# Three of a block's sums of silu(h) on GpSimd, early, in a convolution + silu MLP kernel

## The chip, the cores and the metric

One NeuronCore of a Trainium2 chip. The metric is device time in microseconds of one execution of the whole program; the number to compare is the median of the runs. PE is TensorE, DVE VectorE, ACT ScalarE, POOL GpSimd, SP SyncE (here it only issues DMAs).

## What is computed

The reference, cut to what matters (fp32 throughout):

```python
# x: (8, 4096, 192); weight: (8 heads, 7 taps)
w = softmax(weight, axis=-1)
x_pad = concat([zeros(B, 6, D), x], axis=1)
conv[b, s, h, g] = sum_k w[h, k] * x_pad[b, s + k, h, g]      # causal, 7 taps
x = conv.reshape(32768, 192)
h = x @ w_in                                                  # 192 -> 2048
g = h * (1.0 / (1.0 + np.exp(-h)))                            # silu
out = g @ w_out                                               # 2048 -> 192
```

## The kernel before, in words

**Blocks.** The 32768 tokens are worked on in 32 blocks of 1024 (two halves n of 512). A block goes through: load (`ld`, DMA), transposing into channels by tokens (`i`, DVE), the left edge (`ha`), the convolution (`v`), spreading of its result to other partitions (`sp`, DMA), differences of the spread tiles (`w`, DVE), the products with w_in (`P`, `L`, PE), sums that turn products into h (`u`, `X`, `a`, `b`), silu (`S`, `SL`, ACT), sums of silu(h) (`t`), the products with w_out (`D`, PE), sums of those (`M`, `z`, `y`, `x`), transposing back (`o`) and storing (`st`).

**Products.** Both matrix products use a scheme with fewer multiplications, in which inputs are first added or subtracted and the products are added afterwards. For w_in there are five groups g of 15 products each; P5.2 is product 5 of group 2. A product uses 64 of the 128 rows, so two run at once. Each group has three PSUM banks in which products are added one after another (chains, `CHAINS` in line 618: the first is 5, 2, 6, 1, 0, 14) and two more banks (x banks). Between two products of the first chain ACT copies the bank's present value into an SBUF tile (u5.2 is the copy behind P5.2, in line 698), and the next product of the chain is then added to the same bank, so it waits until the copy has read it. DVE adds such a copy to the second chain's bank: into an x bank (`X`), or into h (`a`), and subtracts the third (`b`), all in line 692. X2.2 is followed by P13.2, which adds to that x bank. `S` applies silu (line 710): S0, S1 and S5 work in place on h in SBUF, S2, S3 and S4 read PSUM. All these run in the first half of a block's time; the w_out products (`D`, line 765, 48 of them) fill the other half.

**The sums of silu(h).** For each quarter j of the 2048 features there are four (lines 718 to 733), 16 in a block, each of 128 x 1024 elements in fp32, both inputs and the output in SBUF. With g(a, n) the silu values of chunk a and half n: t.j0 = g(0,1) - g(0,0); t.j1 = g(1,1) - t.j0; t.j2 = g(1,1) - g(0,1); t.j3 = g(1,0) - t.j1. For j = 0, t.00 reads the results of S0.0, S4.0, S1.0 and S5.0; t.01 and t.02 read those of S3.0 and S1.4 as well. D1 and D0 need no sum; D2.00 is the first that reads t.01, D4.01 and D5.00 read t.00, D3.00 reads t.02. The results go into tiles of the pool `t`, which has three buffers of 128 x 2048.

**The convolution of a later block** runs between all this. For each of three channel groups k and seven taps, `v.k0` is a scaled copy on ACT into the tile nat; `v.k1` to `v.k6` (lines 509 to 513) are a scaled copy on ACT into one of ten tiles u, then a DMA, issued from POOL's queue, that adds that tile to nat. The ten tiles are handed out in the order in which they came back (list `free`): `v` takes one and puts it back at once, `u` takes one and `X` or `a` puts it back. Whoever writes a tile next waits for its last reader, for instance that DMA.

**Order.** Each engine executes in program order. That order is written out by hand in the string `PLAN`, one token after the other for one block, gone through once for each iteration; `-`, `=` and `+` before a token mean one block earlier, two earlier, one later. So in iteration b, `+v.21` is tap 1 of group 2 of the convolution whose result is needed two blocks later, `-t.00` is a sum of the block before. `START` is the same for the first planned blocks (iteration 2), whose w_out products of block 0 run in another form. `finish` (line 937) ends the last block. A k-th instruction of an engine in the trace can thus be matched with a token.

Around the change, PLAN reads (token, engine): S4.4, S0.0 (ACT), +v.21 (ACT, then a DMA from POOL), P5.2 (PE), u5.2 (ACT), P14.4, S3.4, P1.1, u0.1, P13.1, S2.1, P8.4, a0.4 (DVE), P5.3, u5.3, sp.1 (DMA from SP), P2.2 and so on. SP issues, in the same stretch, one of the four DMAs of `sp.1`, three of `-st.1` (stores) and four of `-ld.1` (loads).

```python
    def used(*key):                                   # line 682
        free.append(us.pop(key))
...
            z = free.pop(0)                           # line 510, conv, taps 1 to 6
            pin(nc.scalar.activation(z, src, AF.Copy, scale=tap))
            pin(nc.gpsimd.dma_start(out=dst, in_=z, accum_op=ALU.add))
            free.append(z)
```

Of the kernel before, what the change touches and what calls it, by code (L numbers as in the profile page):

```python
# [12 lines left out]
ALU = mybir.AluOpType  # L13
# [4 lines left out]
def kernel(  # L18
# [24 lines left out]
    nc = tc.nc  # L43
# [36 lines left out]

    PLAN = (
# [21 lines left out]
    )  # L103
    START = (
# [39 lines left out]
    )  # L144
    QUEUE = (0, 4, 1, 2, 3)
    CHAIN_BANKS = (
# [20 lines left out]
    def pin(ins):  # L167
        return tc.keep_in_program_order(ins)
# [37 lines left out]
    x0 = x.flatten_outer_dims()[TB - pad : TB, :].rearrange("t (k c) -> c k t", k=NK)  # L206
# [511 lines left out]
    def sum_g(b, j, i):  # L718

        t = sums.setdefault((b, j), {})  # L720
        if i // 2 not in t:
            t[i // 2] = tpool.tile([P, 2, 2 * TB], F32, tag="t", name="t")

        def of(a, n):
            return gs[b, j, a][:, n, :, :].rearrange("p e t -> p (e t)")

        u, v = (
            (lambda: (of(0, 1), of(0, 0))),
            (lambda: (of(1, 1), t[0][:, 0, :])),
            (lambda: (of(1, 1), of(0, 1))),  # L730
            (lambda: (of(1, 0), t[0][:, 1, :])),
        )[i]()
        pin(nc.vector.tensor_tensor(t[i // 2][:, i % 2, :], u, v, op=ALU.subtract))  # L733

    def out_slot(b, j, i, e, half=None):

# [145 lines left out]
    def step(b, token):  # L882
# [19 lines left out]
        elif name[0] in "uXabS":  # L902
            sums_h(b, name, *digits)
        elif name == "t":
            sum_g(b, *digits)
        elif name[0] == "D":
            i, (j, e) = int(name[1]), digits
            for half in range(2) if i == 3 and b == NB - 1 else (None,):
                out_slot(b, j, i, e, half)
        elif name[0] in "Mzyx":  # L910
            merge(b, name, *digits)
        elif name == "o":
            turn_out(b, *digits)
        elif name == "st":
            store_out(b, *digits)
        elif name == "dp":
            next(downs)
        elif name == "cp":
            copy_plain(b, *digits)
        elif name == "go":  # L920
            pool.tensor_copy(warm, nats[1][:, digits[0], 0, 0:1])
            for g in (2, 3):
                for e in range(2):
                    combine(g, e)
        elif name == "ld":
            if b + 1 < NB:
                load(b + 1, digits)
        elif b + 1 < NB:
            {"i": turn_in, "ha": halo_in, "v": conv, "sp": spread, "w": win}[name](
                b + 1, *digits[: 1 + (name == "v")]  # L930
            )
# [204 lines left out]
```

## Time and profile before

| what | value |
|---|---|
| median of 2 runs | 2319.99 us (2319.82 to 2320.15) |
| the profiled execution's span | 2317.9 us, 2.1 us under that median |
| PE, DVE, ACT, POOL busy | 2310.2, 1797.9, 1496.0, 534.9 us |
| a steady block (P5.1 to the next block's P5.1) | 71.19 us |
| granted TensorE clock, mean | 1.000 |
| sums of silu(h) on DVE, `t<-g`, x248 | mean 1216 ns |
| sums of silu(h) on DVE, `t<-g,t`, x248 | mean 1223 ns |
| silu in place, `g<-g` on ACT, x465 | mean 629 ns |
| convolution DMAs from POOL, `nat<-u`, x504 | mean 947 ns on POOL, landing after 4.5 us (median) |

How to read it: a line of a timeline gives the start in us, the length in us, the engine, the line of the kernel, the operation, output<-input by the program's names, partitions x elements, how many instructions were merged, and in brackets how long the engine had sat idle ahead of it and what ended that. A line of the list of groups gives busy us, mean ns of one, and idle us before them. A matmul's start is the start of its stream; its end is modelled. "Landing" is the time from a DMA's start on its queue to the last of its semaphore updates. An fp32 matmul shows as two instructions. All times in us are counted from the start of the span; most are from the block with u5.2 at 1260.64.

### The profile page before, as it was taken

What the parts mean: (1) busy time and instruction counts of PE and PEld (TensorE: products, weight loads), DVE (VectorE), ACT (ScalarE), POOL (GpSimd) and SP (SyncE); (2) the same over time, 40 slices, a digit from 0 to 9 for tenths busy, and PEclk for the clock granted to TensorE, in tenths of its full rate; (3) what the DMA queues carried; (4) which work ended last, traced back from release to release, by engine and by line L of the source; (5) the groups of instructions that cost most, each with busy time, mean ns of one, the idle gap of its engine ahead of it and who ended that gap; (6) DMA issues with size and microseconds to landing.
All of it is one profiled execution on the core that took longest, in us unless ns stands there. A gap on an engine that the chain in (4) does not pass through costs nothing.

```text
span 2317.9 us, 45421 instructions
## 1 busy us (share of the span) xinstructions
PE 2310.2 (100%) x17630; PEld 949.6 (41%) x17630; DVE 1797.9 (78%) x2373; ACT 1496.0 (65%) x2779; POOL 534.9 (23%) x675
## 2 busy tenths in 40 slices
PE   9999999999999999999999999999999999999999
PEld 5454443444433344433444334443334443344433
DVE  8998777777777777777777777777777777777777
ACT  5347766677666686666776667866667666677543
POOL 4921112221122211222211222112221212221100
PEclk9999999999999999999999999999999999999999
DMA  7236557766567765677655676556776557765401
GB/s 159 58 62 101 98 100 118 123 115 102 95 113 120 121 105 93 109 120 121 110 98 99 115 124 117 102 93 113 119 123 108 94 104 120 120 114 93 81 17 25
DMA packets 522601, 238.81 MB, mean 103 GB/s; under 512 B 430368, under 2 KB 435488, under 8 KB 522384
## 3 DMA queue, kind: packets, MB, share of 16 engines
q0 software_dynamic: 73120, 133.89, 34.4%
q1 hardware_dynamic: 447392, 101.78, 25.0%
q8 instruction: 138, 2.26, 0.4%
q14 instruction: 79, 0.65, 0.1%
q10 hardware_dynamic: 1872, 0.23, 0.1%
HBM read 31.46 MB, written 25.17 MB: 24 GB/s over the span
## 4 chain that ended last, share of the span: by engine, by line
PE 89%; DVE 0%; issue 0%; ACT 0%; ACTq 0%
PE ps L765 45%; PE ps L649 39%; PE ps L666 5%; DVE cmb L175 0%; ACT u L175 0%; DVE osb L175 0%; ACTq L175 0%
## 5 line engine op out<-in xcount | busy, mean ns | idle before, releaser
L512 POOL DMA_DIRECT2D nat<-u x504 | 432.6, 947 | 1544.6 <-ACT u L511 1192.3
L765 PE MATMUL ps<-g,wo 128*32 128x512 f32 x2976 | 694.9, 592 | 0.0
L649 PE MATMUL ps<-win,wr 64*128 64x512 f32 x1550 | 688.7, 591 | 0.8 <-ACT yx L828 0.8
L649 PE MATMUL ps<-win,ws 64*128 64x512 f32 x1550 | 644.3, 589 | 0.0
L698 ACT COPY u<-ps 128x512 f32<-128x512 f32 x775 | 452.2, 587 | 166.8 <-PE ps L649 93.8
L765 PE MATMUL ps<-t,wo 128*32 128x512 f32 (+2 forms) x4528 | 538.5, 446 | 0.0
L765 PE MATMUL ps<-t,wx 128*32 128x512 f32 x2976 | 485.1, 592 | 0.0
L649 PE MATMUL ps<-dup,wr 64*128 64x512 f32 x868 | 425.6, 589 | 0.0
L511 ACT ACTIVATE u<-xt,taps 128x512 f32<-128x512 f32 x504 | 346.0, 715 | 44.0 <-DMA nat<-u 43.6
L733 DVE TENSOR_TENSOR t<-g,t 128x1024 f32<-128x1024 f32 x248 | 303.3, 1223 | 89.7 <-PE ps L765 84.2
L692 DVE TENSOR_TENSOR g<-u,ps 128x512 f32<-128x512 f32 x465 | 312.2, 682 | 72.2 <-PE ps L649 58.8
L649 PEld LDWEIGHTS ps<-win,wr 64*128 64x128 f32 x1550 | 275.7, 187 | 217.1 <-issue 177.1
L733 DVE TENSOR_TENSOR t<-g 128x1024 f32<-128x1024 f32 x248 | 298.8, 1216 | 76.4 <-PE ps L765 56.7
L692 DVE TENSOR_TENSOR ps<-u,ps 128x512 f32<-128x512 f32 x310 | 215.7, 696 | 132.3 <-PE ps L649 62.0
L710 ACT ACTIVATE g<-ps 128x512 f32<-128x512 f32 x465 | 281.0, 604 | 48.6 <-PE ps L649 47.0
L649 PEld LDWEIGHTS ps<-win,ws 64*128 64x128 f32 x1550 | 258.8, 187 | 126.1 <-issue 103.9
L710 ACT ACTIVATE g<-g 128x512 f32<-128x512 f32 x465 | 281.4, 629 | 30.3 <-DVE g L692 30.3
L765 PEld LDWEIGHTS ps<-t,wo 128*32 128x32 f32 x4528 | 181.4, 110 | 239.2 <-issue 227.6
L649 PE MATMUL ps<-dup,ws 64*128 64x512 f32 x682 | 271.9, 589 | 0.0
L831 ACT COPY cmb<-ps 96x512 f32<-96x512 f32 x30 | 17.4, 581 | 393.1 <-PE ps L765 393.1
L765 PE MATMUL ps<-g,wx 128*32 128x512 f32 x1488 | 245.9, 594 | 0.0
L765 PEld LDWEIGHTS ps<-g,wo 128*32 128x32 f32 x2976 | 170.4, 110 | 130.6 <-issue 129.8
(93 smaller groups left out, 2015.1 us busy)
## 6 DMA issues: line engine op xcount, KB each, us to landing
nat<-u POOLq DMA_DIRECT2D x504, 256.0 KB, 4.5
dup<-nat SPq DMA_DIRECT2D x345, 128.0 KB, 2.5
nat<-in_x_dram SPq DMA_DIRECT2D x382, 64.0 KB, 4.4
out_dram<-osb SPq DMA_DIRECT2D x376, 64.0 KB, 2.0
raw<-in_moe_w_out_dram SPq DMA_DIRECT2D x8, 384.0 KB, 3.7
raw<-in_moe_w_in_dram SPq DMA_DIRECT2D x12, 192.0 KB, 4.8
ws<-wr POOLq DMA_DIRECT2D x8, 192.0 KB, 4.8
raw<-in_moe_w_in_dram SPq DMA_DIRECT2D x6, 128.0 KB, 3.1
```

Of the source, the lines that this page charges most:

```text
L511: pin(nc.scalar.activation(z, src, AF.Copy, scale=tap))
L512: pin(nc.gpsimd.dma_start(out=dst, in_=z, accum_op=ALU.add))
L649: nc.tensor.matmul(to[:, cols], raw(g, *LEFT[e][r], e), rhs[:, cols], start=first, stop=True, skip_group_check=True,)
L666: nc.tensor.matmul(plain_bank(b, n and 1 + e)[:, cols], rows(wr[j] if own == e else ws[j], e)[:, a, k, :], rows(dups[b], e)[:, SLOT[e][2 * ...
L692: pin(nc.vector.tensor_tensor(out_, u, v, op=op))
L698: pin(nc.scalar.copy(us[b, g, o][:, cols], t1[:, cols]))
L710: pin(nc.scalar.activation(h, src, AF.Silu))
L733: pin(nc.vector.tensor_tensor(t[i // 2][:, i % 2, :], u, v, op=ALU.subtract))
L765: nc.tensor.matmul(accs[b][at][SQ * q : SQ * q + SQ, to], lhs[:, e, SQ * k : SQ * k + SQ], rhs[:, e, ts(q, TB // 4) if i == 5 else to], st ...
L831: pin(nc.scalar.copy(c[0], acc[0][0:n, :]))
```

## The change

Two things are moved together. First, for blocks 2 and later, the sums t.00, t.01 and t.02 are executed by GpSimd. Second, their tokens stand earlier: in the iteration of their own block, among its products with w_in, instead of in the next iteration among the products with w_out. So that t.00's inputs are there, S1.0 and S5.0 move too, from the next iteration to right behind S0.0. t.03 and the twelve sums of the other quarters stay with DVE at their places. START gets the five tokens at its end; its old `-t.00`, `-t.01`, `-t.02` there belong to block 1 and stay on DVE. The lines of the strings are broken anew; the tokens that change are these:

```diff
 PLAN
-... -a5.3 -P8.1 -S5.0 -S1.0 -a1.2 -S3.2 ...
+... -a5.3 -P8.1 -a1.2 -S3.2 ...
-... -D1.00 =st.3 -t.00 -b5.3 ...
+... -D1.00 =st.3 -b5.3 ...
-... -D0.31 -D1.10 -t.01 -t.03 -D2.00 -sp.0 -b5.2 -t.02 -D4.01 ...
+... -D0.31 -D1.10 -t.03 -D2.00 -sp.0 -b5.2 -D4.01 ...
-... S4.4 S0.0 +v.21 P5.2 u5.2 ...
+... S4.4 S0.0 S1.0 S5.0 t.00 +v.21 P5.2 u5.2 ...
-... P10.1 S1.4 a5.1 P3.3 ...
+... P10.1 S1.4 t.02 t.01 a5.1 P3.3 ...
 START
-... u0.3 -st.1 +v.00 P9.3 b5.1
+... u0.3 -st.1 +v.00 P9.3 b5.1 S1.0 S5.0 t.00 t.02 t.01
 sum_g
-        pin(nc.vector.tensor_tensor(t[i // 2][:, i % 2, :], u, v, op=ALU.subtract))
+        engine = nc.gpsimd if b > 1 and j == 0 and i < 3 else nc.vector
+        pin(engine.tensor_tensor(t[i // 2][:, i % 2, :], u, v, op=ALU.subtract))
```

87 rows, old and new, of tables (PLAN, START) are left out of this document.

## Prediction

> **What bounds the kernel now.** I read the page first (engines, chain that ended last), then the chain in order of time, then timelines of ACT, POOL, DVE and PE over one steady block. Page, parts 1 and 4:
>
> ```profile
> PE 2310.2 (100%) x17630; PEld 949.6 (41%) x17630; DVE 1797.9 (78%) x2373; ACT 1496.0 (65%) x2779; POOL 534.9 (23%) x675
> PE 89%; DVE 0%; issue 0%; ACT 0%; ACTq 0%
> ```
>
> A busy PE is not yet a bound (ends of matmuls are modelled), so the chain in order of time (start, length, what) decides:
>
> ```profile
> 1249.31 30.04 PE ps L649 x140
> 1279.35 36.22 PE ps L765 x384
> ...
> 1320.50 30.04 PE ps L649 x140
> 1350.54 36.22 PE ps L765 x384
> ```
>
> Stretch for stretch the same, 71.19 us a block. In the PE timeline two 512-column matmuls, one for each half of the rows, start every 0.43 us through the whole block, at a granted clock of 1.00. Nothing but PE's own work sets the period, and DVE's 78% lies beside it. What the change takes from DVE can save nothing in a block; it can only cost, where it makes a matmul wait. So I look for slack on what is moved. The ACT timeline of the stretch where the new tokens go; in the order of PLAN these are S0.0, v.21, u5.2, S3.4, u0.1, S2.1, u5.3, and, after lines left out, u2.2:
>
> ```profile
> 1259.51 0.63 ACT L710 ACTIVATE g<-g 128x512 f32<-128x512 f32 x1
> 1260.03 0.72 ACT L511 ACTIVATE u<-xt,taps 128x512 f32<-128x512 f32 x1
> 1260.64 0.58 ACT L698 COPY u<-ps 128x512 f32<-128x512 f32 x1
> 1261.11 0.61 ACT L710 ACTIVATE g<-ps 128x512 f32<-128x512 f32 x1
> 1261.60 0.60 ACT L698 COPY u<-ps 128x512 f32<-128x512 f32 x1
> 1262.06 0.63 ACT L710 ACTIVATE g<-ps 128x512 f32<-128x512 f32 x1
> 1262.55 0.62 ACT L698 COPY u<-ps 128x512 f32<-128x512 f32 x1
> ...
> 1266.51 0.58 ACT L698 COPY u<-ps 128x512 f32<-128x512 f32 x1 [0.23 <-PE ps L649]
> ```
>
> No gap from 1259.51 to 1262.55: ACT is full just here. POOL has time, but what it does is DMA for the convolution (v.21, then v.01):
>
> ```profile
> 1261.04 0.84 POOL L512 DMA_DIRECT2D nat<-u  x1 [15.74 <-ACT u L511]
> 1274.83 0.85 POOL L512 DMA_DIRECT2D nat<-u  x1 [12.95 <-ACT u L511]
> ```
>
> **The change, part by part.**
>
> *Off DVE:* three sums of 1.22 us, 3.7 us a block, in the output products. Before, t.01 ended at 1282.19 and D2.00 began at 1284.45; DVE had 2.3 us in hand there and PE waited for none of the three. Gain 0.
>
> *The two silus moved on ACT (S1.0, S5.0).* They ran at 1275.36 and 1275.89, just as close together as S0.0 and its successor (0.53 and 0.52 us from start to start), so they push what follows back by 1.05 us. u5.2 then ends at 1260.64+1.05+0.58 = 1262.27. P2.2 adds to the bank that u5.2 reads, and started at 1262.02. How soon a matmul follows its releaser is seen in block 15, the one steady block where a late DVE sum held PE (period 71.203 against 71.188); DVE, then PE:
>
> ```profile
> 1126.51 0.70 DVE L692 TENSOR_TENSOR ps<-u,ps 128x512 f32<-128x512 f32 x1 [0.49 <-ACT g L710]
> ```
> ```profile
> 1127.35 0.60 PE L649 MATMUL ps<-dup,wr 64*128 64x512 f32 x1
> ```
>
> 0.14 us after the end at 1127.21. So P2.2 starts at 1262.41, 0.39 late. u5.3, pushed equally, ends at 1263.60+0.60 = 1264.20; P2.3 needs its bank, starts at 1264.34 instead of 1263.73: 0.61 late in all (not added: one stream). By 1265.7 ACT's idle pieces (0.2 to 0.3 us each) have eaten the 1.05 and nothing else is reached. At their old place the silus leave a hole that saves nothing, as PE did not wait there.
>
> *t.00 on POOL, ahead of v.21's DMA.* It needs S5.0, which ends at 1260.56+0.63 = 1261.19. POOL follows ACT by 0.29 us (v.21: ACT ended 1260.75, POOL 1261.04): t.00 starts at 1261.48. A sum of 1024 elements on POOL isn't in the trace; the nearest rows are the weight combinations near 110 us:
>
> ```profile
> L175 POOL TENSOR_TENSOR wr<-ws 64x128 f32<-64x128 f32 x2 | 0.9, 452 | 0.2
> L175 POOL TENSOR_TENSOR wx<-wx,wo 128x192 f32<-128x192 f32 x4 | 2.4, 592 | 0.3
> ```
>
> 64 more elements cost 140 ns, 2.19 ns each; from 192 to 1024 that adds 1.82 us: 2.41 us. From below, the same sum on DVE, 1.22; from above, 192 elements taken five and a third times, 3.16. I take 2.41, the line through two rows of the same engine. Beside DVE's three-operand L516 the 452 became 0.9 us, beside L692, which alone (with transposes) runs in these windows, it did not change; so no surcharge. The Trainium skill (GPSIMD Engine Reference, section 3.1) gives 4497 ns for 2048 elements, by which an estimate is 2.25 us; the landing below would come 0.16 earlier and the block's price would be 0.64 instead of 0.80, the total 2342.
>
> The DMA of v.21 then starts at 1263.89 instead of 1261.04. It landed 3.5 to 3.6 us after its start in 24 of 27 blocks (4.3 to 4.9 in the other three). At the new time it shares the engines with three stores and four loads of 64 KB that SP issues from 1264.45 to 1267.52 (DMA share 0.54 and 0.48 there). From below 3.3, the best of this DMA's kind; from above 4.9, v.01, which goes out beside the spreads (share 0.71). I take 3.8: near its own row, as its transfer met 128 KB of spreading before too. It lands at 1267.69. Its source tile comes back from the list of the ten u tiles at u2.2, which follows from the order of takes and returns in PLAN. That such a copy waits for the DMA, and that ACT resumes 0.06 us after the landing, shows a block earlier in u5.0 (v.03 landed at 1224.81):
>
> ```profile
> 1224.87 0.58 ACT L698 COPY u<-ps 128x512 f32<-128x512 f32 x1 [0.88 <-DMA nat<-u]
> ```
>
> So u2.2 starts at 1267.75, not 1266.51: 1.24 late. X2.2 on DVE follows its end directly (1267.10 to 1267.13 before), ends at 1269.07, and P13.2 starts at 1269.21 instead of 1268.45: 0.76, say 0.80 with what queues behind u2.2 on ACT (S1.4, u2.3, and through u2.3 X2.3, which has 0.36 in hand). This takes the place of the 0.61, being on the same stream. Formula: landing time less 3.0 us, but never under 0.61.
>
> *t.02 and t.01 on POOL:* S1.4 moves to 1268.2 to 1268.9; the two sums run from 1269.2 to 1274.0, before v.01's DMA (1274.83 plus the stall) and ten us before D2.00. Price 0; if the sums took 3.2 us, v.01 would still go out within a microsecond of its time.
>
> *The first planned block.* In START the five tokens stand at the end, behind v.00. S1.0 and S5.0 push S4.2 from 203.68 to 204.73 on ACT, and P12.3 (204.87, on the bank that S4.2 reads until 205.35) is 0.6 late. All three sums come at once on POOL, 204.7 to 211.9, and v.01's DMA, at 206.18 before, stands behind them; with its 4.6 us it lands at 216.5. u5.4 takes that tile and was at 211.09: 5.4 late. S0.3 is behind it on ACT, and D0.31 started 0.14 after S0.3 ended. Once, 5.4 us; from below 0.6, if a part of the sums runs beside the DMA's descriptors, from above 7, if DMAs pile up.
>
> *Extra waits:* a D that reads POOL's sum waits for one more semaphore, some 0.02 us of PE's sequencer, hidden behind the running matmul.
>
> **Sum.** v.21 exists in iterations 3 to 29, 27 of them; in 30 and 31 u5.2 has 0.57 us of idle time ahead of it and the push is absorbed. 27 x 0.80 + 5.4 = 27.0. The profiled execution spans 2317.9, 2.1 under the median of the runs, 2319.99; the increment is put on the median: 2347. Own range: 27 x 0.61 + 0.6 = 17, so 2337, up to 1.45 a block, 2365.
>
> **Rivals.**
> *Slower by over 2%.* One mechanism: v.21's DMA loses against SP's stores and loads. 2% is 46.4 us; less 5.4 that is 1.52 a block, reached when the landing takes over 4.5 us. With v.01's 4.9 it is 1.9 x 27 + 5.4 = 57: 2377. For it: v DMAs beside loads landed after 5.6 to 6.5 us in the output stage. Against: those stood behind another DMA of their own queue, v.21 stands alone. 0.17.
> *Nothing reaches PE:* 2320. It needs over 1.05 us in hand at P2.2 and P2.3, where I count 0.65 and 0.42. 0.07.
> *DVE was the bound after all:* 3.7 us in each of 30 blocks, 2210. The Trainium skill (Perfetto Trace Analysis, Identifying the Most-Contended Engine) judges TensorE by LDWEIGHTS busy, here 41%, which would put DVE's 78% first; by that rule this case would come. The trace disagrees: equal starts every 0.43 us. 0.02, any gain included.
>
> **Numbers.** Likeliest 0.74, with 2347. The range leaves out the cases at 2320 and below (0.09) and the upper half of the slow case (0.09): 2332 to 2372. Within 2%, about what a measurement of this kernel can tell from no change: 0.74 + 0.07 = 0.81; slower 0.17, faster 0.02.
>
> **What would show it.** Right: block period about 72.0; ACT with two L710 g<-g more right behind S0.0; PE gaps of 0.4 before P2.2, 0.2 before P2.3, 0.2 before P13.2; POOL sums of 2.4 us; u2.2 waiting for DMA nat<-u; one hole of about 5 us near 213 us. Wrong: a period of 71.19 (slack misread), a landing over 4.5 us, POOL sums over 3 us, or PE waiting for a POOL sum in the output products.

## The result, and the profile after

| what | before | after |
|---|---|---|
| median of 2 runs each | 2319.99 us | 2342.27 us (2342.26 to 2342.28) |
| ratio to before, 95% interval | | 1.0097 (1.0068 to 1.0127) |
| span of the profiled execution | 2317.9 us | 2340.2 us |
| most steady blocks (P5.1 to P5.1) | 71.19 us | 71.82 us |
| granted TensorE clock, mean | 1.000 | 1.000 |

About 1% slower, 22.3 us; predicted were 2347 us, "within 2%". Page of the changed kernel, parts 1 and 4 (busy us of each engine; shares of the chain that ended last):

```profile
PE 2326.2 (99%) x17630; PEld 959.7 (41%) x17630; DVE 1698.7 (73%) x2283; ACT 1493.1 (64%) x2779; POOL 745.9 (32%) x765
PE 83%; ACT 5%; issue 1%; DMA 0%; DVE 0%; POOLq 0%; POOL 0%; ACTq 0%
```

DVE lost 99 us of work and the program became longer. ACT, absent from the chain before, has 5% of it now. Where, the chain in order of time shows, in the block of after that answers to the one shown of before (start, length, what):

```profile
1262.92 8.64 PE ps L650 x40
...
1272.75 2.04 ACT g L711 x4
1274.79 0.61 ACT u L512
1275.40 0.48 ACT u L699
...
1275.93 17.67 PE ps L650 x80
```

The stretch of 30.04 us in which PE waited for nothing is broken once. The piece in the middle is read backwards: PE goes on at 1275.93 (P2.2) when the copy u5.2 (L699) is done, which stood behind v.21 (L512), which stood behind four silus (L711). Two of those four are the ones that were moved, as the ACT timeline shows; the first line is S0.0, S1.0 and S5.0 merged, the third u5.2:

```profile
1273.13 1.67 ACT L711 ACTIVATE g<-g 128x512 f32<-128x512 f32 x3
1274.69 0.72 ACT L512 ACTIVATE u<-xt,taps 128x512 f32<-128x512 f32 x1
1275.30 0.58 ACT L699 COPY u<-ps 128x512 f32<-128x512 f32 x1
```

P5.2, ahead of all this on PE, started at 1259.44 before and at 1273.06 after: this block lies 13.62 later when the stretch begins. Measured against that, u5.2 is 1.04 late (14.66 - 13.62). A product shows as two instructions on its half of the rows, one beat of 0.43 apart. The PE timeline on P2.2's half, first before (P5.3's second instruction, P2.2's first), then after (the same two, and P2.2's second):

```profile
1261.60 0.59 PE L649 MATMUL ps<-dup,wr 64*128 64x512 f32 x1
1262.02 0.59 PE L649 MATMUL ps<-win,wr 64*128 64x512 f32 x1
```
```profile
1275.21 0.59 PE L650 MATMUL ps<-dup,wr 64*128 64x512 f32 x1
1275.93 0.69 PE L650 MATMUL ps<-win,wr 64*128 64x512 f32 x1
...
1276.46 0.59 PE L650 MATMUL ps<-win,wr 64*128 64x512 f32 x1
```

P2.2 (1275.93) comes 0.72 after P5.3's second instruction instead of one beat, 0.30 late; its own second instruction comes 0.53 after the first, another 0.10 late. P9.1, beside it on the other half, has the same two delays. At the pair of P2.3 (behind u5.3) and P12.1 another 0.12 is lost, and again 0.10 at their second instructions. Together 0.63 us, the same in all 27 iterations from 3 to 29 (0.30, 0.10, 0.12 and 0.10 on the mean); iterations 30 and 31, which have no v.21, lose nothing, as the prediction said.

GpSimd in the same block: t.00, then v.21's DMA; and its sums in the list of groups (busy us, mean ns of one, idle us before):

```profile
1274.93 2.35 POOL L735 TENSOR_TENSOR t<-g 128x1024 f32<-128x1024 f32 x1 [16.00 <-ACT g L711]
1277.24 0.86 POOL L513 DMA_DIRECT2D nat<-u  x1
```
```profile
L735 POOL TENSOR_TENSOR t<-g 128x1024 f32<-128x1024 f32 x60 | 141.2, 2355 | 626.7 <-ACT g L711 545.5
```

That DMA landed after 3.4 us in 21 of the 27 blocks, and u2.2 started at 1280.76: 14.25 later than before, of which 13.62 + 0.63 = 14.25 was there already. So here the DMA added nothing. In six blocks it did. Block 8, the chain:

```profile
628.98 5.03 DMA nat<-u
...
634.08 0.59 ACT u L699
...
634.72 5.29 PE ps L650 x20
```

v.21's DMA took 5.03 us, u2.2 followed 0.08 behind its end, and PE restarted behind u2.2 with P1.2, which adds to the bank that u2.2 reads. X2.2 then ended at 635.40 and P13.2 started at 635.45, later still. Blocks 5, 7, 8, 11, 21 and 27 (landings 4.2, 3.7, 5.0, 3.8, 3.5, 3.8) lose 1.10, 0.84, 2.17, 0.95, 0.69 and 0.91 us, together 2.9 more than 0.63 each.

The steps of block 8 give the loss as a formula. The DMA starts 4.17 after P5.2; u2.2 follows the landing by 0.08; X2.2 ends 1.32 after u2.2's start; P13.2 starts 0.05 after that, where before it started 8.58 after P5.2; its second instruction loses 0.10 more. So a block loses the landing less 2.86, where that is over 0.63: 2.17, 0.83, 0.96, 0.69 and 0.90 for blocks 8, 7, 11, 21 and 27. Block 5 gives 1.31, of which the kernel before had 0.20 already (71.39 there against 71.19). In the 21 other blocks (landings 3.37 to 3.44) the formula stays under 0.63.

The first planned block. Three sums back to back on POOL (204.20 to 211.22), v.01's DMA behind them at 211.15 instead of 206.18. ACT, u5.4, and DVE, t.10:

```profile
216.24 0.59 ACT L699 COPY u<-ps 128x512 f32<-128x512 f32 x1 [4.99 <-DMA nat<-u]
```
```profile
221.39 1.22 DVE L735 TENSOR_TENSOR t<-g 128x1024 f32<-128x1024 f32 x1 [7.45 <-ACT g L711]
```

ACT sat 4.99 us at u5.4 until the DMA had landed. All that follows it on ACT is late, S0.1 by 4.66 (220.74 against 216.08); t.10 and t.11 on DVE wait for that; D2.11 started at 223.93, 0.06 after t.11's end, 1.84 late. P12.3, a little earlier, lost the 0.6 that S4.2 was pushed by. 2.5 us, once.

All of it: 27 x 0.63 = 17.0 for the silus, 2.9 for six late landings, 2.5 at the start, less 0.25 by which the program's beginning was shorter: 22.2 of 22.3 us.

### The profile page after: what moved, and what is told of

Same layout as the page of the kernel before. It is cut to its first block, busy times and chain, and to the rows that moved or that the text cites. A ratio compares the mean times of both kernels' runs of the same rounds, so it can differ in the third digit from the quotient of the medians.

```text
span 2340.2 us, 45533 instructions
## 1 busy us (share of the span) xinstructions
PE 2326.2 (99%) x17630; PEld 959.7 (41%) x17630; DVE 1698.7 (73%) x2283; ACT 1493.1 (64%) x2779; POOL 745.9 (32%) x765
## 4 chain that ended last, share of the span: by engine, by line
PE 83%; ACT 5%; issue 1%; DMA 0%; DVE 0%; POOLq 0%; POOL 0%; ACTq 0%
PE ps L767 45%; PE ps L650 34%; PE ps L667 5%; ACT g L711 2%; ACT nat L509 1%; ACT u L512 1%; ACT u L699 1%; DMA nat<-u 0%; DVE cmb L176 0%; ACT u L176 0%; DVE osb L176 0%; POOL t L735 0%; POOLq L513 0%; POOLq L735 0%; ACTq L176 0%
## 5 line engine op out<-in xcount | busy, mean ns | idle before, releaser
L650 PE MATMUL ps<-win,ws 64*128 64x512 f32 x1550 | 656.6, 593 | 0.5 <-ACT u L699 0.5
L699 ACT COPY u<-ps 128x512 f32<-128x512 f32 x775 | 449.5, 592 | 164.1 <-PE ps L650 82.7
L512 ACT ACTIVATE u<-xt,taps 128x512 f32<-128x512 f32 x504 | 347.4, 716 | 63.1 <-DMA nat<-u 63.0
L735 DVE TENSOR_TENSOR t<-g,t 128x1024 f32<-128x1024 f32 x218 | 266.7, 1224 | 110.2 <-PE ps L767 105.7
L735 POOL TENSOR_TENSOR t<-g 128x1024 f32<-128x1024 f32 x60 | 141.2, 2355 | 626.7 <-ACT g L711 545.5
L711 ACT ACTIVATE g<-ps 128x512 f32<-128x512 f32 x465 | 280.2, 603 | 78.0 <-PE ps L650 77.4
L735 DVE TENSOR_TENSOR t<-g 128x1024 f32<-128x1024 f32 x188 | 225.8, 1216 | 129.8 <-ACT g L711 73.6
L711 ACT ACTIVATE g<-g 128x512 f32<-128x512 f32 x465 | 274.0, 624 | 8.8 <-DVE g L693 8.8
```

Source lines behind the costliest of these rows:

```text
L650: nc.tensor.matmul(to[:, cols], raw(g, *LEFT[e][r], e), rhs[:, cols], start=first, stop=True, skip_group_check=True,)
L699: pin(nc.scalar.copy(us[b, g, o][:, cols], t1[:, cols]))
L711: pin(nc.scalar.activation(h, src, AF.Silu))
L735: pin(engine.tensor_tensor(t[i // 2][:, i % 2, :], u, v, op=ALU.subtract))
```

## The experiments

Theory before them: the price per block is the push of ACT by the two silus, and the DMA behind t.00 costs only where it lands late. Rival: the sum on GpSimd is what costs (its DMA, or its sharing of SBUF), and the silus are harmless. A second question was whether DVE's relief is worth anything. Each kernel's time stands beside a run of the kernel before on the same chip (2319.5 to 2320.0 throughout); an experiment was run once unless a number of runs is given.

### Only the silus moved, sums untouched

```diff
 PLAN   (from before)
-... -P8.1 -S5.0 -S1.0 -a1.2 ...
+... -P8.1 -a1.2 ...
-... S4.4 S0.0 +v.21 P5.2 u5.2 ...
+... S4.4 S0.0 S1.0 S5.0 +v.21 P5.2 u5.2 ...
 START
-... P9.3 b5.1
+... P9.3 b5.1 S1.0 S5.0
```

> Only S1.0 and S5.0 are moved (behind S0.0, and to START's end); all sixteen sums stay on VectorE at their old places. Theory A (the two silus push ACT by 1.05 us where it is full, u5.2 and u5.3 come late, PE waits 0.63 us a block): 27 blocks with v.21 lose 0.63 us each, the first planned block another 0.63 at P12.3: 2320 + 17.6 = about 2338, block period 71.82, and no wait of u2.2 for a DMA. Theory B (GpSimd's sums cost it, by their place ahead of v.21's DMA): 2320.

Measured 2337.34 (before: 2319.60), +17.7. The same stalls, 27 times: 0.30 at P2.2 and P9.1, 0.10 at their second instructions, 0.12 and again 0.10 at P2.3 and P12.1, and 0.6 once at P12.3. No sum ran on GpSimd. u2.2 was 0.62 to 0.63 late; only in block 5 did it start later, 0.71, behind v.21's landing, which had not been expected. So 17.7 of the 22.3 us come from moving two silus of 0.6 us each, which the change needs only to have t.00's inputs early.

### Only one silu moved

```diff
 PLAN   (from before)
-... -P8.1 -S5.0 -S1.0 -a1.2 ...
+... -P8.1 -S1.0 -a1.2 ...
-... S4.4 S0.0 +v.21 ...
+... S4.4 S0.0 S5.0 +v.21 ...
 START
-... P9.3 b5.1
+... P9.3 b5.1 S5.0
```

> Only S5.0 is moved behind S0.0, S1.0 and all sums stay. Theory A with the slacks counted in the prediction (0.65 us ahead of P2.2, 0.42 ahead of P2.3): one silu pushes by 0.53 us, P2.2 keeps its time, P2.3 starts 0.11 late: 27 x 0.11 = 3, so 2323. If the cost went with the number of silus instead of with slack used up, it would be half of 17, 2329. Theory B: 2320.

Measured 2323.18 (2319.60), +3.6. P2.2 is on time; what is left is 0.12 a block, 0.10 of it at the second instruction of P2.3 and P12.1. The chain of this kernel has the block's first part in one piece again:

```profile
1251.27 30.16 PE ps L647 x140
```

30.16 instead of 30.04. Half of the push costs a fifth, so what decides is slack. It can now be counted out: u5.2 ended 0.80 before P2.2's turn, u5.3 0.56 before P2.3's (1262.02 - 1261.22; 1263.73 - 1263.17), and PE follows ACT by 0.05 (1275.88 to 1275.93). One silu (0.52) is just over 0.56 - 0.05; two (1.04) are over both.

### The DMA ahead of t.00

```diff
 PLAN   (from after)
-... S0.0 S1.0 S5.0 t.00 +v.21 P5.2 ...
+... S0.0 S1.0 S5.0 +v.21 t.00 P5.2 ...
```

> The changed kernel with t.00 one token later, behind v.21, so that v.21's DMA goes out ahead of the sum. Theory A: the 0.63 us a block stay, and only what blocks 5, 7, 8, 11, 21 and 27 lost beyond that (u2.2 waiting for v.21's landing, 2.9 us together) goes: 2339.4. Theory B: most of the 22 us go, 2320 to 2325.

Measured 2340.44 (2319.60), 1.8 less than after. v.21's DMA no longer waits for the sum, and the 0.63 a block is unchanged: the DMA is not its cause. Of the six blocks with more, two are left: 5 with 1.28 and 27 with 1.12, where this DMA took 5.2 and 5.5 us; elsewhere it took 4.0 to 4.7. D2.11's stall at the start is there with 1.46, since v.01's DMA still stands behind three sums.

### The first planned block as before

```diff
 PLAN   (from after; a silu or sum already done is passed over)
-... -P8.1 -a1.2 ...      -D1.00 =st.3 -b5.3 ...
+... -P8.1 -S5.0 -S1.0 -a1.2 ...      -D1.00 =st.3 -t.00 -b5.3 ...
-... -D1.10 -t.03 -D2.00 -sp.0 -b5.2 -D4.01 ...
+... -D1.10 -t.01 -t.03 -D2.00 -sp.0 -b5.2 -t.02 -D4.01 ...
 START
-... P9.3 b5.1 S1.0 S5.0 t.00 t.02 t.01
+... P9.3 b5.1
 sum_g
-        engine = nc.gpsimd if b > 1 and j == 0 and i < 3 else nc.vector
+        engine = nc.gpsimd if b > 2 and j == 0 and i < 3 else nc.vector
```

> The changed kernel, but block 2's two silus and three sums are done as before, in iteration 3 and on VectorE; from block 3 on as changed. Theory A: the first planned block's 0.63 us at P12.3 and 1.84 us at D2.11 go, the rest stays: 2342.3 - 2.5 = 2339.8. If those two holes came from elsewhere (the later convolution DMAs of START), 2342.

Measured 2339.89 (2319.60), 2.4 less than after. The stalls at P12.3 and D2.11 are gone, the 0.63 a block is there, and blocks 5, 7, 8 and 11 again have late landings (4.6, 3.7, 4.9, 4.2).

### The silus where ACT has gaps

```diff
 PLAN   (on top of the experiment before)
-... S4.4 S0.0 S1.0 S5.0 t.00 +v.21 P5.2 ...
+... S4.4 S0.0 +v.21 P5.2 ...
-... P12.1 u1.1 P7.1 b5.4 u4.3 P11.1 ...
+... P12.1 u1.1 S1.0 P7.1 b5.4 u4.3 S5.0 t.00 P11.1 ...
```

> From the changed kernel: S1.0 goes behind u1.1 and S5.0 with t.00 behind u4.3, where ACT sits idle for 0.2 to 0.3 us before each copy, and block 2 is done as before. t.00 then stands behind v.21's DMA. Theory A: u5.2 and u5.3 are in time again, u4.3 and S4.1 come about 0.2 to 0.3 us late and have 0.7 us in hand, so nothing reaches PE: 2320 (2319 to 2321), block period 71.19, with the three sums still on GpSimd at 2.35 us each. Theory B (the sums on GpSimd cost time by themselves): clearly above 2320, up to 2337.

Measured 2319.95 (11 runs; 2319.42 to 2320.26) against 2319.51 (15 runs) of before: ratio 1.0001 (0.9992 to 1.0010). Page and chain:

```profile
PE 2310.7 (100%) x17630; PEld 944.9 (41%) x17630; DVE 1698.9 (73%) x2286; ACT 1489.1 (64%) x2779; POOL 735.9 (32%) x762
```
```profile
1036.15 30.04 PE ps L647 x140
1066.19 36.22 PE ps L764 x384
```

All 87 sums of blocks 3 and later still run on GpSimd, DVE is at 73%, and PE's stretches in a steady block are those of before to the hundredth. The sums on GpSimd cost nothing where they delay no transfer that is needed soon, and taking 3.7 us a block off DVE gains nothing.

### One sum twice on DVE

```diff
 sum_g  (from before)
-        pin(nc.vector.tensor_tensor(t[i // 2][:, i % 2, :], u, v, op=ALU.subtract))
+        for _ in range(2 if b > 1 and j == 0 and i == 0 else 1):
+            pin(nc.vector.tensor_tensor(t[i // 2][:, i % 2, :], u, v, op=ALU.subtract))
```

> The kernel before with t.00 of blocks 2 to 31 executed twice on VectorE (the second time to the same place), 1.22 us more VectorE work in each block's output products. Theory A (VectorE's time there is worth nothing, t.01 has 2.3 us in hand): 2320. If VectorE's time counted in the block at all: up to 1.22 x 30 = 37 more, 2357.

Measured 2320.11 (2319.51). The page:

```profile
PE 2310.2 (100%) x17630; PEld 952.7 (41%) x17630; DVE 1834.5 (79%) x2403; ACT 1496.1 (65%) x2779; POOL 531.4 (23%) x675
```

37 us more on DVE and PE's 2310.2 unchanged, the period too. With the experiment before, DVE was moved both ways, by 3.7 us less and 1.2 us more a block, and the time stood still: DVE is not the bound. The Trainium skill (Perfetto Trace Analysis, Identifying the Most-Contended Engine) judges TensorE by MFU (the share of its peak that the kernel reaches) and by LDWEIGHTS busy; by the second, 41%, it would have named DVE, and here the measurement decides against that.

### Only the engine changed, nothing moved

```diff
 sum_g  (from before; PLAN and START untouched)
-        pin(nc.vector.tensor_tensor(t[i // 2][:, i % 2, :], u, v, op=ALU.subtract))
+        engine = nc.gpsimd if b > 1 and j == 0 and i < 3 else nc.vector
+        pin(engine.tensor_tensor(t[i // 2][:, i % 2, :], u, v, op=ALU.subtract))
```

> Only the engine is changed: the three sums go to GpSimd at their old places in the next iteration, silus as before. Theory A: GpSimd's queue is in order and full of the convolution's DMAs there; t.01 stands behind v.23's DMA (before: 1288.8 us in the block whose D2.00 started at 1284.45), so D2.00 waits 7.5 us and more in each of 30 blocks: over 2530. If GpSimd's 77% idle time were what counts: 2320 to 2325. VectorE's sums with two SBUF inputs run beside GpSimd's there; if they hold each other up, GpSimd's sums take longer than 2.35 us.

Measured 2630.28 (2319.51), +310.8, a block of about 82.3 us. The view of waits (engine, line, what it waited for: us in total, times, longest) and t.03 in the DVE timeline:

```profile
PEld ps L766 <- POOL t L734: 252.0, 29, 9.9
```
```profile
1131.03 3.37 DVE L734 TENSOR_TENSOR t<-g,t 128x1024 f32<-128x1024 f32 x1 [11.85 <-POOL t L734]
```

POOL's queue has the convolution's DMAs between the sums. v.23's copy was done on ACT at 1121.06, but its DMA started only at 1127.78, 0.5 us after the landing (1127.25) of v.22's, which adds to the same part of nat; t.01 started behind it at 1128.34, and D2.00 had to wait until 1131.05. So the early place matters: POOL executes in order, and at the old place a sum stands behind DMAs that wait and comes too late for PE.

The rest of the 310.8 is mostly clock. In 28 blocks the granted clock fell to 0.50 for 6.8 or 10.2 us (here 1128.16 to 1134.99), 3 to 6 us after the start of PE's last matmul ahead of the wait, and the matmuls from D2.00 on started 0.84 apart instead of 0.43 until it ended. The matmuls begun in these stretches fill 53 us at 0.43 each, so about 53 us were lost there (an estimate from the starts in the trace).

### t.00 twice on GpSimd

```diff
 sum_g  (from after)
-        pin(engine.tensor_tensor(t[i // 2][:, i % 2, :], u, v, op=ALU.subtract))
+        for _ in range(2 if engine is nc.gpsimd and i == 0 else 1):
+            pin(engine.tensor_tensor(t[i // 2][:, i % 2, :], u, v, op=ALU.subtract))
```

> The changed kernel with t.00 executed twice on GpSimd, so that v.21's DMA goes out another 2.35 us later and nothing else on ACT or PE's lists changes. Theory A with the chain of the prediction (landing, u2.2, X2.2, P13.2): in block 17 the DMA would start at 1279.6 and land at 1283.0; u2.2, at 1280.75 in the changed kernel, comes 2.3 us late, X2.2 has 0.49 us in hand ahead of P13.2, so each of 27 blocks loses another 1.8 us (2.4 in all), and the first planned block's hole at D2.11 grows by 2.35: 2342.3 + 49 + 2.4 = 2394. If the late DMA does not reach PE by that chain (the six slow blocks had another cause): 2342 to 2345.

Measured 2446.39 (2319.97); the chain as expected, its size not: 126 us more than before, where 74 were expected. POOL and ACT (u2.2) in a block:

```profile
1334.14 4.80 POOL L736 TENSOR_TENSOR t<-g 128x1024 f32<-128x1024 f32 x2 [16.01 <-ACT g L711]
1338.89 0.85 POOL L513 DMA_DIRECT2D nat<-u  x1
```
```profile
1343.33 0.58 ACT L699 COPY u<-ps 128x512 f32<-128x512 f32 x1 [3.58 <-DMA nat<-u]
```

v.21's DMA now lands after 3.2 to 4.9 us (3.9 or more in 26 of 27 blocks) instead of 3.4, and u2.2 waits for it in every block; here 3.58 us. PE stands ahead of P1.2, and then of P13.2. The DMA starts 2.43 later after P5.2 than in the changed kernel, so the formula becomes landing less 0.43: 3.94 in this block (landing 4.37), 2.81 in block 29 (3.24); measured 3.94 and 2.82. The expected 1.8 was too low by the longer landing and because X2.2 (1282.07) had 0.21 in hand ahead of P13.2's first instruction (1282.28 in the changed kernel), not 0.49. The DMA chain of the prediction thus exists. In the changed kernel it lies at the edge, hidden behind the silus' stall in most blocks.

18 of the 27 blocks cost 2.8 to 4.4 us more than before, the other nine 4.9 to 7.1. In these nine, and once ahead of them, the granted clock was 0.50 for 3.4 or 6.8 us, from the time when PE stood or up to 1.7 us after it. The view of windows for block 7 (stretch; its length; busy time and instructions of PE, PEld, DVE, ACT, POOL; clock; DMA share; GB/s):

```profile
585.40:592.21 6.81, 6.44 (x15) 3.81 (x17) 3.81 (x6) 3.04 (x7) 4.66 (x2) 0.50 0.00 0
```

The matmuls begun in the ten stretches fill 21 us at 0.43 a beat, so about 21 of the 126 us are this clock (an estimate from the starts in the trace). Three things were added here, then: a later start, a longer landing, and the clock. The longer landing is put down to the stores and loads that SP issues in the same microseconds (1337.68 to 1340.94), which was not tried by itself.

## Why the prediction was right, and where it was not

- *PE sets the time, DVE's relief is worth 0:* right, shown from both sides (DVE at 73% and at 79%, same time). The rivals at 2210 and at 2320 did not come.
- *The two silus push ACT by 1.05:* right, 1.04. P2.2 0.39 and P2.3 0.61 late in all: 0.30 and 0.53 measured, since PE follows ACT by 0.05, not by 0.14. The 0.14 was no wait: the matmul at 1127.35 (P13.3) started on its beat, 1.72 after P13.2 as in the block before, and what followed DVE's end at 1127.21 was its weight load, at 1127.26. Then 0.10 twice at second instructions; the 0.10 at P2.2's is within the 0.53, the last is in no term. 0.53 + 0.10 = 0.63: the near match with 0.61 is two errors that cancel.
- *v.21's DMA behind t.00, 0.80 a block in place of 0.61:* the path was right, its sizes were off both ways. The inputs were each a little high: sum 2.355 us (2.41 taken; the estimate of 2.25 by the Trainium skill's GPSIMD Engine Reference, section 3.1, is 0.1 low), start 0.14 after S5.0 (0.29 taken, which is what a DMA needs, not a sum), landing 3.4 (3.8 taken). The formula, landing less 3.0, was too low for its inputs: it takes P13.2 to start at 1268.45, which is its second instruction. Both, in the PE timeline of before:

```profile
1268.03 0.59 PE L649 MATMUL ps<-dup,wr 64*128 64x512 f32 x1
...
1268.45 0.59 PE L649 MATMUL ps<-dup,wr 64*128 64x512 f32 x1
```

X2.2 ended at 1267.83, 0.20 ahead of the first. From 1268.03 the prediction's own steps give 1.18 a block, and 2357 in all. That 0.80 lies near the 0.74 measured on the mean (19.9 over 27 blocks) is luck: the misread start and the high inputs pull against each other. From the measured steps the formula is landing less 2.86; at 3.4 the floor of the silus' stall rules, so the silus alone set 21 of 27 blocks, and the six others follow the formula. The sum had 21.6 us for the blocks; they cost 17.0 + 2.9 = 19.9.

- *Slower rival, landing over 4.5 us in every block:* did not come; 5.0 us in one block of 27. That the mechanism is real and near, t.00 done twice showed.
- *The first planned block, 5.4 us:* the step that failed. "S0.3 is behind it on ACT, and D0.31 started 0.14 after S0.3 ended" took a coincidence in time for a dependence. In after, D0.31 starts at 213.94 while S0.3 starts at 217.96: D0.31 does not read S0.3. All up to u5.4 was right (5.15 late at 216.24), but the first product that needed something behind it was D2.11, by S0.1, t.10 and t.11, and it had 2.8 us in hand, counted at its place in the changed kernel. 2.5 in place of 5.4, the P12.3 stall of 0.6 included.
- *t.02 and t.01 early on POOL, and the extra waits, at 0:* right; with the silus in the gaps they run at the same place and the time is that of before.

Left open: why just these six blocks have a late v.21, and what the 0.10 at the second instruction of a product that waited is made of.

## What to carry to other kernels

Moving work to an idle engine is worth its time only if the engine relieved is what the others wait for; before that question, look at what has to be moved along so that the inputs are there, because here two small silus on a full stretch of ACT cost 17.7 of 22.3 us, and the moved sums the rest, through the DMAs behind them. Slack is a threshold: one silu cost 3.6 us, two 17.7, and the same two in ACT's gaps nothing. On an in-order queue that also issues DMAs, ask which copy gets its buffer back from the DMA that now starts later, and confirm a dependence in the code before a start that follows an end by 0.14 us is taken for one. Where a product shows as two instructions, count what it has in hand from the first.

## What the runs showed of the hardware

- How soon a successor starts depends on the pair: PE 0.05 us after ACT and 0.05 to 0.06 after DVE (P13.2 in block 8, D2.11), a sum on POOL 0.14 after ACT, a DMA on POOL 0.29 after ACT.
- The first instruction of a product that waited shows 0.69 us instead of 0.59, and its second comes 0.53 after it instead of 0.43. P2.2's two weight loads start at 1275.93 and 1276.04; P8.4's second, ahead of it, starts with P8.4's first matmul (1274.78, 1274.77), and its second matmul follows at 1275.20.
- The same 256 KB DMA (v.21) landed after 3.5 to 3.6 us in 24 of 27 blocks of the kernel before, 3.4 in 21 of 27 when started 2.6 us later (counted from P5.2), 4.0 to 4.1 in 22 of 27 when started 1 us later (DMA ahead of t.00), 3.2 to 4.9 when 5.0 later (t.00 twice). That is not a rising function of the delay; what the transfer meets on its way is the likely cause, which was not tried.
- A sum of 1024 elements with both inputs in SBUF takes 2.36 us on GpSimd and 1.22 on DVE. Beside each other they do not share: in the kernel with only the engine changed, DVE's t.03 starts 0.38 us behind POOL's t.02 in 28 blocks and ends 1.09 us behind it, 3.37 us long, about the rest of t.02 and a whole sum of its own. That agrees with the Trainium skill (SBUF — State Buffer, Who interferes with whom): the second to start is blocked until the first is done. POOL's t.02 shows 2.65 us there, but so does t.01, beside which DVE ran nothing, and the two records overlap by 0.34, so this length is not DVE's doing. In the changed kernel the sums on GpSimd run beside DVE instructions with at most one input in SBUF, and neither got longer (2355 ns on GpSimd; on DVE 683 ns for `g<-u,ps`, 682 in the kernel before).
- The granted clock fell to 0.50 for 3.4, 6.8 or 10.2 us where PE had stood: in 28 blocks with stands of 7.6 to 9.5 us from start to start (only the engine changed; mean clock 0.959, PE busy 91%), and ten times with stands of 2.5 to 5.1 us (t.00 twice; 0.991, 97%). In other blocks of the second kernel PE stood about as long without it (2.9 us in block 17); what decides was not tried. The other kernels had a mean of 0.999 or 1.000.
